# A fused attention and feed-forward kernel: eight of tile 3's twelve gate and val chunks as seven half-size products, with the program behind the opening written out in a new order

## The chip, the cores and the metric

The kernel runs on one core of a Trainium2 chip. The metric is the time of one execution in device microseconds (us); shown are 3 runs of the kernel before, from 216.14 to 217.49, with a median of 216.69. The time covers everything from the inputs in DRAM to the output in DRAM. Besides the times there is one execution recorded by the hardware profiler; its span, from the first to the last instruction, is shorter than the time, because start and end of the program are outside it.

## The reference

Attention with a decay per head, in blocks of 64 rows with a running state, then a gated feed-forward layer on its output:

```python
q, k, v: [4, 8, 768, 64]      lam: [8]         # batch, head, row, head_dim; fp32
for b in range(nb):                            # blocks of 64 rows, per batch and head
    intra = (qb @ kb.T * Dmask) @ vb           # Dmask = lam**(i-j) where i >= j, else 0
    inter = (qb * lam**(pos+1)) @ kv_state
    out[block] = intra + inter
    kv_state = lam**64 * kv_state + (kb * lam**(63-pos)).T @ vb
x = out, with heads side by side               # [3072, 512]
g = x @ w_gate;  v = x @ w_val                 # [3072, 1536]
result = (g * sigmoid(g) * v) @ w_out          # [3072, 512]
```

## The kernel before

**Tiles, groups, chunks.** The 3072 tokens are six tiles of 512 (t = 0 to 5). A tile is two groups, and a group is 256 rows of one batch; group g belongs to tile g // 2, and its state goes on to the group of the same batch four later. The attention of group g writes half of `xt` of its tile (bf16, d_model on the partitions). The feed-forward part of a tile cuts d_ff = 1536 into twelve chunks of 128 (`FC` = 12, two halves of `FH` = 6): for each chunk a gate product (L585) and a val product (L603), four pieces of d_model each, then SiLU on ScalarE (L590) and the product `h = sil * val` on VectorE (L607). Then the output product with `w_out` follows.

**Seven products instead of eight.** Where a matrix product is cut into two by two quarters, it can be had from seven products of quarters instead of eight, with sums of quarters made ahead and sums of results made behind. The kernel does so for the output product of tiles 1 to 5 (`out_units`, L805; its products `p1` to `p7`, L834 to L865, all matmuls at L823) and for the gate and val products of tiles 4 and 5 (`ffn_unit`, L716). The sums ahead are

- sums of the weights: `w_combo` (L681, the operation at L696), for gate and val n = 0, 1, 2, in `ws`; n = 3 overwrites a quarter of the weights in place, so after it no ordinary product can use that quarter. Sums of `w_out`: `wo_combo` (L644);
- sums of x: `x_combo` (L702, the operation at L714), four for a tile, three into `xs`, the fourth in place in `xt`;
- sums of h: `h_combo` (L655, the operation at L670), four for the chunks that are done, three into `hs`, one in place in `h`.

A call `ffn_unit(t, j, bk, ...)` makes four chunks at once: 2j, 2j+1 and the two six further on. Its seven products come one behind the other, each for gate (i = 0) and then for val (i = 1); a group of products is four matmuls of 256 columns at L733, so a unit has 7 x 2 x 4 = 56. It works in six of the eight PSUM banks, called A, E and B in pairs. The steps:

```python
        for i in range(2):
            product(i, A[i], wa(0, 0), xb(0, 0), True)
            nc.scalar.copy(out=Bb[i], in_=A[i])
        for i in range(2):
            product(i, E[i], wa(0, 1), xb(0, 1), True)
            nc.scalar.copy(out=es[i], in_=E[i])
        for i in range(2):
            product(i, Bb[i], wsum(1), xsum(1))
            nc.vector.tensor_tensor(out=E[i], in0=Bb[i], in1=es[i], op=ALU.add)
```

Then the product on A with `xb(1, 0)` and its SiLU; the product on B with `wsum(0), xsum(0)` and the addition of B and `es` into `es` (L783); the product on E with `xsum(2)`; the product on B with `wsum(2)`. The copies are L767 and L770, the additions L775 and L783, the SiLU L760, and `mult` (L763) makes h, three times on VectorE and once on GpSimd. So a group on E may begin only when its bank has been copied to `es` by ScalarE and rewritten by VectorE's addition.

**The attention of a group**, in steps which are functions: loads of q, k and v on SyncE's queue (`load_fp32`); `cast_scaled` (L287: k to bf16 on ScalarE, q times its decay factor on VectorE, and then `dma_transpose`, L276, which issues on SyncE's queue the DMA that transposes both into `qkt`); `v_scale` (L263: v times a decay factor, GpSimd or VectorE); `scores` (L362, L392) with masks on VectorE (L369, L397) that are collected in `later`; `upd_mm` (L424), `upd_copy` (L446, ScalarE) and `state` (L479 to L483, GpSimd) for the running state; `inter` (L518), `guard` (L502) and `intra` (L531) for the output of the group; `evac` (L544, L547) from PSUM to `xt`. The matmuls of scores, state and output are of 64 rows, those of the feed-forward part of 128.

**What sets the order.** The program is written in one order, and each engine runs its instructions in that order. The opening (groups 0 and 1 and the start of tile 0) is written out. Behind it `steps` lists the chunks tile by tile, `plan` (filled by `at`) hangs attention steps, loads and sums behind chosen chunks, and three lists hand out small work: `later` (masks), `trickle` by `drip` (sums of h, x and weights), and `kvq` by `kv_flush` (copies of the state). Tile 1 runs in halves of 256 columns, and so do the first four chunks of tile 2; chunks 4 and 5 of tile 2 are `HALVED`, each product split in two. Tile 3 takes its chunks in the order 0, 1, 6, 7, 2, 3, 8, 9, 4, 5, 10, 11, all twelve as ordinary chunks of 512 columns. `WS` (L1131) places the sums of the weights: two behind late chunks of tile 1, two in tile 2, and those with n = 2 and n = 3 in tile 3. The four sums of x for tile 4 are handed out during the output product of tile 2. From L1201 to the end the tail is written out: output of tile 2, units (4,0) and (4,1) with the attention of groups 10 and 11 in and between them, output of tile 3, unit (4,2), units (5,0) and (5,1), output of tile 4, unit (5,2), output of tile 5.

**Buffers.** The eight PSUM banks are given by a ring (`bank`, with `set_bank` and `fixed`). The pools touched: `raw` 10 (raw loads, sums of h, weight sums of the output), `qk` 3, `qkt` 3 (also sums of x of tile 4), `v` 4, `h` 5, `sil` 4, `osb` 4, and four `ups`/`es` buffers of 128 x 512 fp32.

## Time and profile before

| | us |
|---|---|
| median of the runs (216.14 to 217.49) | 216.69 |
| span of the profiled execution | 215.0 |
| VectorE busy | 148.3 |
| ScalarE busy | 130.9 |
| GpSimd busy | 92.7 |

Busy time of each engine by stretch of the span (us). PE is TensorE's matmuls; the stretches are, in turn: the opening, tile 0 and most of tile 1; the end of tile 1, first chunks of tile 2 and, from 69.3, the output product of tile 0 with the attention of group 5; tile 2 with the output product of tile 1; tile 3; the output product of tile 2 with units (4,0) and (4,1) and their attention, then the output product of tile 3; the units (4,2), (5,0), (5,1), (5,2) and the output products of tiles 4 and 5.

| stretch | length | PE | VectorE | ScalarE | GpSimd |
|---|---|---|---|---|---|
| 0 to 60 | 60.0 | 56.64 | 34.18 | 40.78 | 36.34 |
| 60 to 82 | 22.0 | 21.84 | 18.10 | 9.24 | 14.55 |
| 82 to 108 | 26.0 | 25.98 | 17.99 | 13.86 | 16.68 |
| 108 to 135.4 | 27.4 | 27.40 | 21.87 | 20.36 | 11.00 |
| 135.4 to 168.7 | 33.3 | 33.30 | 28.49 | 21.77 | 9.48 |
| 168.7 to 215 | 46.3 | 42.97 | 27.72 | 24.93 | 4.66 |

A row of the timeline or of the groups names engine, line, operation, the output and the inputs by the program's names, and partitions x elements; PE's ends are modelled, so its starts are the safer figure. Matmuls overlap: the time from one group's start to the next group's start is what a group costs.

### The profile page before, as it was taken

How to read it: one execution, taken by the hardware profiler on the slowest of the kernel's cores; microseconds unless marked ns; L12 is line 12 of the kernel's file. 1: busy time of each engine (PE TensorE's matmuls, PEld its weight loads, DVE VectorE, ACT ScalarE, POOL GpSimd, SP SyncE). 2: the span in 40 equal slices, each digit the busy share in tenths (PEclk: the TensorE clock that was granted, in tenths of full speed). 3: DMA queues.
4: the chain of work that ended last, by engine and by line, in shares of the span. 5: the costliest groups of instructions: out<-in, count | busy, mean ns of one | idle time of the engine just before them, and what ended most of it. 6: DMA issues, size and time to landing. Idle time of an engine off the chain costs nothing.

```text
span 215.0 us, 6856 instructions
## 1 busy us (share of the span) xinstructions
PE 208.1 (97%) x2797; PEld 153.3 (71%) x2801; DVE 148.3 (69%) x267; ACT 130.9 (61%) x280; POOL 92.7 (43%) x128
## 2 busy tenths in 40 slices
PE   8789999999999999999999999999999999999993
PEld 3467445887888548866754545888888888888883
DVE  1773447576677989874569878697988389961940
ACT  5878676756636153638369487774983676636522
POOL 6675755818399440595962153240750022200200
PEclk9999999999999999999999999999999999999999
DMA  6999999999999778899576859855000500005014
GB/s 188 345 354 381 376 336 296 285 226 223 309 387 174 185 212 208 244 214 263 122 198 143 217 121 257 207 121 201 5 3 5 195 0 3 0 0 198 0 52 146
DMA packets 82176, 39.76 MB, mean 185 GB/s; under 512 B 45410, under 2 KB 77794, under 8 KB 82146
## 3 DMA queue, kind: packets, MB, share of 16 engines
q1 hardware_dynamic: 80946, 38.74, 64.7%
q10 hardware_dynamic: 1200, 0.59, 0.9%
q8 instruction: 22, 0.36, 0.7%
q14 instruction: 8, 0.07, 0.1%
HBM read 28.31 MB, written 6.29 MB: 161 GB/s over the span
## 4 chain that ended last, share of the span: by engine, by line
PE 93%; DMA 2%; DVE 1%; SPq 1%; ACT 0%; issue 0%; DVEq 0%
PE bank L823 22%; PE bank L585 20%; PE bank L603 19%; PE bank L733 17%; PE bank L623 5%; PE bank L531 3%; DMA kraw<-in_k_dram 2%; PE bank L518 2%; PE bank L424 2%; PE bank L362 1%; DVE ssb L369 1%; SPq L115 1%; PE bank L392 1%; PE bank L322 1%; ACT qk L306 0%
## 5 line engine op out<-in xcount | busy, mean ns | idle before, releaser
L607 DVE TENSOR_TENSOR h<-sil,bank 128x256 bf16<-128x256 bf16 (+1 forms) x67 | 35.0, 533 | 29.9 <-PE bank L603 17.2
L585 PE MATMUL bank<-xt,wg_sb 128*128 128x256 bf16 (+1 forms) x276 | 52.8, 315 | 0.0
L603 PE MATMUL bank<-xt,wv_sb 128*128 128x256 bf16 (+1 forms) x276 | 52.5, 314 | 0.0
L590 ACT ACTIVATE sil<-bank 128x256 bf16<-128x256 f32 (+1 forms) x67 | 31.6, 481 | 21.8 <-PE bank L585 18.4
L603 PEld LDWEIGHTS <-wv_sb 128*128 128x128 bf16 x276 | 26.9, 98 | 14.8 <-POOL wv_sb L249 0.2
L585 PEld LDWEIGHTS <-wg_sb 128*128 128x128 bf16 x276 | 25.9, 98 | 13.6 <-issue 0.2
L266 POOL TENSOR_TENSOR v_s<-v,dec 128x512 bf16<-128x512 f32 (+1 forms) x18 | 23.0, 1295 | 24.3 <-DMA v<-in_v_dram 17.3
L763 POOL TENSOR_TENSOR h<-sil,es 128x512 bf16<-128x512 bf16 x6 | 7.0, 1165 | 47.4 <-ACT sil L760 47.4
L823 PEld LDWEIGHTS <-h 128*128 128x128 bf16 x240 | 23.3, 98 | 3.4 <-issue 0.3
L823 PE MATMUL bank<-wo_sb,h 128*128 128x256 bf16 x180 | 21.5, 273 | 0.0
L823 PEld LDWEIGHTS <-hs 128*128 128x128 bf16 x180 | 17.6, 98 | 2.7
L369 DVE TENSOR_TENSOR ssb<-bank,causal 128x512 bf16<-128x512 f32 x24 | 15.4, 684 | 1.8 <-PE bank L362 1.8
L479 POOL TENSOR_TENSOR kvf<-kvs,ups 128x256 f32<-128x256 f32 x8 | 6.5, 814 | 20.9 <-ACT ups L446 20.9
L733 PEld LDWEIGHTS <-ws 128*128 128x128 bf16 x144 | 13.8, 98 | 1.8
L823 PE MATMUL bank<-wt,hs 128*128 128x256 bf16 x120 | 15.0, 273 | 0.0
L775 DVE TENSOR_TENSOR bank<-bank,es 128x512 f32<-128x512 f32 x12 | 7.8, 694 | 9.6 <-PE bank L733 9.6
L479 POOL TENSOR_TENSOR kvf<-kvf,ups 128x256 f32<-128x256 f32 x16 | 13.0, 815 | 0.9
L760 ACT ACTIVATE sil<-bank 128x512 bf16<-128x512 f32 x18 | 10.5, 596 | 3.7 <-PE bank L733 3.7
L733 PE MATMUL bank<-xs,ws 128*128 128x256 bf16 x96 | 12.6, 273 | 0.0
L763 DVE TENSOR_TENSOR h<-sil,bank 128x512 bf16<-128x512 bf16 x18 | 11.8, 683 | 0.3 <-ACT sil L760 0.3
L623 PE MATMUL bank<-wo_sb,h 128*128 128x512 bf16 x45 | 10.7, 380 | 0.2
L733 PE MATMUL bank<-xt,wg_sb 128*128 128x256 bf16 x72 | 10.8, 273 | 0.0
(119 smaller groups left out, 360.3 us busy)
## 6 DMA issues: line engine op xcount, KB each, us to landing
out_dram<-osb SPq DMA_DIRECT2D x22, 256.0 KB, 2.6
v<-in_v_dram SPq DMA_DIRECT2D x18, 256.0 KB, 4.6
woraw<-in_moe_w_out_dram SPq DMA_DIRECT2D x6, 512.0 KB, 7.1
kraw<-in_k_dram SPq DMA_DIRECT2D x24, 128.0 KB, 3.4
qraw<-in_q_dram SPq DMA_DIRECT2D x24, 128.0 KB, 3.4
wraw<-in_moe_w_gate_dram SPq DMA_DIRECT2D x5, 512.0 KB, 6.9
wraw<-in_moe_w_val_dram SPq DMA_DIRECT2D x5, 512.0 KB, 7.0
kraw<-in_k_dram SPq DMA_DIRECT2D x4, 512.0 KB, 6.3
```

The lines of the kernel that those rows point to most:

```text
L266: eng.tensor_tensor(out=st[("vs", g)][:, h0:h1], in0=st[("v", g)][:, h0:h1].rearrange("p h (s d) -> p h s d", s=2), in1=vfac(g, h0, h1), o ...
L369: nc.vector.tensor_tensor(out=ssb[:, h2, 2 * c:2 * c + 2].rearrange("p a s n -> p a (s n)"), in0=sp[(c, h2)].rearrange("p (a x) -> p a x", ...
L479: nc.gpsimd.tensor_tensor(out=o, in0=f, in1=u, op=ALU.add)
L585: nc.tensor.matmul(gp[:, n0:n1], wg_sb[:, mc, fs], xt[:, g0:g1, mc].rearrange("p g b n -> p g (b n)"), start=(mc == 0 and n0 == 0), stop=( ...
L590: nc.scalar.activation(sil[:, 0:N], gp[:, 0:N], AF.Silu)
L603: nc.tensor.matmul(vp[:, n0:n1], wv_sb[:, mc, fs], xt[:, g0:g1, mc].rearrange("p g b n -> p g (b n)"), start=(mc == 0 and n0 == 0), stop=( ...
L607: nc.vector.tensor_tensor(out=h_sb[:, fc % FH, b0:b1].rearrange("p b n -> p (b n)"), in0=sil[:, 0:N], in1=vp[:, 0:N], op=ALU.mult)
L623: nc.tensor.matmul(ps, st[("h", t, fc // FH)][:, fc % FH, b], wo_sb[:, fc, c0:c1], start=(fc == 0), stop=(fc == FC - 1))
L733: nc.tensor.matmul(o[:, fi * 256:fi * 256 + 256], lhs(i, c, 2 * j + fi), rhs(c), start=(start and fi == 0 and c == 0), stop=(c == KH - 1), ...
L760: nc.scalar.activation(sil[key], src, AF.Silu)
L763: eng.tensor_tensor(out=h_of(half, r), in0=v3(sil[half, r]), in1=v3(src), op=ALU.mult)
L823: nc.tensor.matmul(o, lhs(f), rhs(f), start=(start and f == 0), stop=(f == FH - 1), skip_group_check=True)
```

## The change

**Tile 3.** Chunks 0, 1, 6, 7 and 2, 3, 8, 9 become units (3,0) and (3,1) of seven products; 4, 5, 10, 11 stay ordinary. So `ws` of all three kinds and the overwriting n = 3 for these chunks must be done before tile 3, and tile 3 gets sums of x, the fourth into a place of its own since ordinary chunks of the tile still read `xt`:

```diff
-    XS0 = 4
+    XS0 = (3, 4)
...
-            xs[t] = pool.tile([128, 3, 2, KH, BLK], BF16, name="xs", tag=tag)
+            xs[t] = pool.tile([128, 4 if t == 3 else 3, 2, KH, BLK], BF16, name="xs", tag=tag)
...
-    HALVED = ((2, 4), (2, 5))
+    HALVED = ((2, 10), (2, 11))
```

**Small functions.** `ffn_unit` and `out_units` are taken apart, so that each product group can stand anywhere in the program: `unit(t, j, bk)` names the banks, `uprod(t, j, k, i)` is product k for gate or val with the copy or addition that belongs to it, `silu` and `mu` are its SiLU and multiplication; `out_new`, `oprod` and `store` do the same for the output product; `cast_scaled` becomes `kcast`, `qcast` and `dma_transpose`, `h_combo` becomes `hsum` (k = 0 to 3), `core_a`, `core_b` and `attend` become `op_new`, `inter`, `guard`, `intra` and `evr`; `mask` and `kvc` are single steps. `hsum`, `x_combo` and `w_combo` take an engine:

```diff
+    def uprod(t, j, k, i):
...
+        o, lhs, rhs = ((A, wa(0, 0), xb(0, 0)), (E, wa(0, 1), xsum(3) if t == 3 else xb(0, 1)), (Bb, wsum(1), xsum(1)),
+                       (A, wa(1, 0), xb(1, 0)), (Bb, wsum(0), xsum(0)), (E, wa(1, 1), xsum(2)),
+                       (Bb, wsum(2), xb(1, 1)))[k]
...
+        if k == 0:
+            nc.scalar.copy(out=Bb[i], in_=A[i])
+        if k == 1:
+            nc.scalar.copy(out=es[i], in_=E[i])
+        if k == 2:
+            nc.vector.tensor_tensor(out=E[i], in0=Bb[i], in1=es[i], op=ALU.add)
+        if k == 4:
+            nc.vector.tensor_tensor(out=es[i], in0=Bb[i], in1=es[i], op=ALU.add)
```

**The order.** `steps`, `plan`, `at`, `trickle` and the tail go, and everything behind the opening is a list of calls; `use(...)` names the banks of the next step. Tile 2 now runs chunks 6 to 9 in halves first, then 10 and 11 (halved products), then 0 to 5. The sums of the weights all move ahead of tile 3. The casts of q of groups 6 and 11 go to GpSimd, the cast of k of group 7 and the v scaling of group 6 to VectorE. From the end of tile 2 to the output of tile 2:

```diff
+    use(4, 5); op_new(7)
+    use(0, 1); scores(8)
+    inter(7, True)
+    use(6, 7); upd_mm(8)
...
+    use(2); ffn_gate(2, 5, 0, 4)
+    intra(7, False)
+    state(8)
+    evr(7, 1, ACTC)
+    w_combo(1, 3, (0, 2))
+    mask(8, 0, 0)
+    evr(7, 0, DVEC)
+    mask(8, 0, 1)
+    x_combo(3, 0, None)
+    x_combo(3, 3, None)
+    use(7); ffn_val(2, 5, 0, 4)
+    x_combo(3, 1, None, nc.gpsimd)
+    hsum(2, 0, 0, 4, 0, 2)
+    unit(3, 0, (0, 1, 5, 3, 4, 2))
+    uprod(3, 0, 0, 0)
+    uprod(3, 0, 0, 1)
+    uprod(3, 0, 1, 0)
+    uprod(3, 0, 3, 0)
+    silu(3, 0, 0, 0)
+    x_combo(3, 2, None)
+    uprod(3, 0, 2, 0)
+    uprod(3, 0, 1, 1)
+    uprod(3, 0, 2, 1)
+    kcast(9)
+    uprod(3, 0, 4, 0)
+    qcast(9, nc.vector)
+    dma_transpose(9)
...
+    uprod(3, 0, 3, 1)
+    uprod(3, 0, 4, 1)
+    uprod(3, 0, 5, 1)
+    uprod(3, 0, 5, 0)
...
+    mu(3, 0, 1, 1, nc.gpsimd)
+    v_scale(9, nc.gpsimd, 0, 4)
+    hsum(2, 1, 0, 4, 0, 2)
+    mu(3, 0, 0, 0)
+    uprod(3, 0, 6, 0)
...
+    unit(3, 1, (0, 5, 6, 3, 4, 7))
+    uprod(3, 1, 0, 0)
+    uprod(3, 1, 0, 1)
+    uprod(3, 0, 6, 1)
+    uprod(3, 1, 1, 0)
...
+    mu(3, 1, 0, 1)
+    hsum(2, 2, 4, 6, 0, 2)
+    hsum(2, 2, 0, 4, 0, 2)
+    use(3, 2); op_new(8)
+    use(6); ffn_gate(3, 4, 0, 4)
+    inter(8, True)
...
+    use(4, 5); scores(9)
+    use(0, 1); upd_mm(9)
+    kcast(10)
...
+    qcast(10, nc.vector)
+    use(7); ffn_val(3, 4, 0, 4)
+    dma_transpose(10)
...
+    use(2, 5); scores(10)
```

Unit (3,0) so has an order of its own: product 3 for gate stands before product 2, and product 2 for gate before product 1 for val. In the units of tiles 4 and 5 the order of the products stays much as it was; the sums of h and x and the additions around them move, some to GpSimd.

More of the change, by code (lines that the diff above doesn't have):

```diff
@@ new lines, in oprod @@
+        for f in range(FH):
+            nc.tensor.matmul(o, lhs(f), rhs(f), start=(k in (1, 7) and f == 0), stop=(f == FH - 1),
+                             skip_group_check=True)
+        if k == 1:
+            act(out=Bb, in_=A)
+        if k == 7:
+            act(out=es, in_=E)
+        if k == 2:
+            act(out=O[0][:, 0:HD], in_=A)
+        if k == 6:
+            nc.vector.tensor_tensor(out=E, in0=Bb, in1=es, op=ALU.add)
+        if k == 5:
+            nc.vector.tensor_tensor(out=O[1][:, HD:DM], in0=Bb, in1=es, op=ALU.add)
@@ new lines, in _body @@
+    w_combo(0, 0, (0, 3))
+    use(2); ffn_gate(2, 9, 0, 2)
+    use(6); ffn_val(2, 9, 0, 2)
+    w_combo(1, 0, (0, 3))
+    wo_combo(1)
+    use(4); ffn_out(0, 0)
+    use(5, 6); op_new(5)
+    inter(5, True)
+    kcast(6)
+    guard(5)
+    use(7, 0, 1, 2); scores(5)
+    mask(5, 1, 1)
+    mask(5, 1, 0)
+    mask(5, 0, 1)
+    mask(5, 0, 0)
+    use(3); ffn_out(0, 1)
+    intra(5, False)
+    qcast(6, nc.gpsimd)
+    evr(5, 0, DVEC)
+    dma_transpose(6)
+    load_fp32(7, nc.sync, k, "kraw")
@@ new lines, in _body @@
+    store(1, 0, 0, 0, 512, None)
+    w_combo(1, 1, (0, 3))
+    w_combo(0, 2, (0, 3))
+    w_combo(0, 3, (0, 2))
+    use(4); ffn_val(2, 1, 0, 4)
+    use(5, 6); op_new(6)
+    inter(6, True)
+    guard(6)
+    use(7, 0); upd_mm(7)
+    upd_copy(7)
+    use(3, 2); scores(7)
+    intra(6, False)
+    state(7)
+    v_scale(8, nc.gpsimd, 0, 4)
+    use(1); ffn_gate(2, 2, 0, 4)
+    w_combo(1, 2, (0, 3))
+    mask(7, 0, 0)
+    use(7); ffn_val(2, 2, 0, 4)
+    kcast(8)
+    mask(7, 0, 1)
+    evr(6, 0, DVEC)
@@ new lines, in _body @@
+    hsum(3, 1, 0, 4, 0, 2)
+    unit(4, 0, (2, 4, 3, 5, 6, 7))
+    uprod(4, 0, 0, 1)
+    uprod(4, 0, 0, 0)
+    uprod(4, 0, 1, 1)
+    uprod(4, 0, 1, 0)
+    uprod(4, 0, 2, 0)
+    uprod(4, 0, 2, 1)
+    use(0, 1); scores(11)
+    mask(11, 0, 1)
+    uprod(4, 0, 3, 0)
+    silu(4, 0, 0, 0)
+    uprod(4, 0, 3, 1)
+    uprod(4, 0, 4, 0)
+    uprod(4, 0, 4, 1)
+    uprod(4, 0, 5, 1)
+    mu(4, 0, 0, 0)
+    silu(4, 0, 1, 1)
+    uprod(4, 0, 5, 0)
+    silu(4, 0, 1, 0)
+    mask(11, 0, 0)
+    use(2, 1); op_new(10)
```

1175 lines of the change are left out of this document (714 added, 461 removed).

## The prediction

> **What bounds the kernel now.** I read the page first, then the chain of waits in order of time, then the waits of TensorE, then the shapes of each line, and last the timeline around a seven-product unit.
>
> ```profile
> span 215.0 us, 6856 instructions
> PE 208.1 (97%) x2797; PEld 153.3 (71%) x2801; DVE 148.3 (69%) x267; ACT 130.9 (61%) x280; POOL 92.7 (43%) x128
> PE   8789999999999999999999999999999999999993
> PEclk9999999999999999999999999999999999999999
> ```
>
> PE is busy 97% of the span, its clock is full throughout, and what is idle lies in the opening (the first slices) and in the last slice. The waits of PE over the span add up to 3.2 us in seven rows; asked for the stretch from 60 us to the end, the same view has no row. The chain of waits shows the pace:
>
> ```profile
> 97.47 0.38 PE bank L518 x32
> 97.84 0.27 PE bank L424 x30
> 98.11 0.32 PE bank L392 x31
> 98.43 0.32 PE bank L531 x32
> 98.75 0.97 PE bank L585 x4
> 99.71 0.86 PE bank L603 x4
> ...
> 113.60 0.86 PE bank L585 x4
> 114.47 0.86 PE bank L603 x4
> 115.33 0.86 PE bank L585 x4
> ...
> 168.68 18.43 PE bank L733 x168
> ```
>
> An ordinary chunk of 512 columns is four gate and four val products of 0.216 us each: 113.60 to 115.33 is 1.73 us, wall to wall. The last row is three units of tiles 4 and 5: 168 products of 256 columns in 18.43 us, 0.110 us each. So PE streams without pause, and only two things can move the end: fewer columns on PE, or a wait that is not there now. The built order of the two kernels is the same on PE up to the scores of group 4 (about 60 us here), so the opening and its waits stay, and so does the 3.3 us between the last product and the end. The profiled execution took 215.0 us; the median of the runs is 216.69, so 1.69 is added to every span below.
>
> **The change, part by part.**
>
> Columns on PE. Eight chunks of tile 3 cost 8 x 1.73 = 13.84 us. They become two units of 56 products: 2 x 18.43/3 = 12.29 us. Saved: 1.55 us. That the change really issues fewer columns is seen in its order: 64 products of 512 columns go, 112 of 256 come, every other PE shape keeps its count.
>
> One more switch. PE changes between full and 64-row products 56 times after, 54 before; a chunk behind such a block takes 0.97 instead of 0.86 (98.75 against 113.60). One more visit, in and out: 0.11 to 0.2, taken as 0.15.
>
> Work around the units. The rows I use:
>
> ```profile
> L770 ACT COPY es<-bank 128x512 f32<-128x512 f32 x12 | 6.6, 612 | 0.0
> L775 DVE TENSOR_TENSOR bank<-bank,es 128x512 f32<-128x512 f32 x12 | 7.8, 694 | 9.6 <-PE bank L733 9.6
> L763 POOL TENSOR_TENSOR h<-sil,es 128x512 bf16<-128x512 bf16 x6 | 7.0, 1165 | 47.4 <-ACT sil L760 47.4
> ```
>
> and from the timeline of a unit of tile 4 (start, us, engine, line, operation):
>
> ```profile
> 168.51 0.60 PE L733 MATMUL bank<-xt,wg_sb 128*128 128x256 bf16 x4
> 168.95 0.60 PE L733 MATMUL bank<-xt,wv_sb 128*128 128x256 bf16 x4
> 169.21 1.06 ACT L767 COPY bank<-bank 128x512 f32<-128x512 f32 x2
> ```
>
> In the first three, the figure behind the comma is the mean in ns. A product group of four takes 0.44 (168.51 to 168.95); its reader starts 0.10 after its modelled end (169.11 to 169.21), so 0.26 after the next group has begun. A DVE operation that follows another directly costs its duration less 0.08 to 0.09.
>
> VectorE loses eight h products (8 x 0.685) and gains, for two units, six multiplications of 0.683 and eight additions of 0.69, a net gain of work of 4.1 us; with three sums of x for tile 3 and what is passed between engines, its rows add up to about 6 more on 148. GpSimd takes two casts of q (1.9 each), four sums of x, three of h and one of weights, and two multiplications of 1.17, and gives up 4.2 of v scaling. Sums on GpSimd are in no row here; the nearest is the 1165 ns row (same 512 elements), the ends are 0.72 (an addition of kvf, 256) and 2.1 (a v scaling of 1024), and I take 1.0 to 1.2. Together about 10 more on 93. ScalarE's rows add up to the same. No engine gets near PE, so none of this costs by amount; it costs by place.
>
> Place one, the way into unit (3,0). In tile 4 the sums of x run beside 84 products of output work (135.39 to 144.56). Now only one val group of 512 columns, 0.86 + 0.11, stands between the last product of group 7's attention and the unit. VectorE must evacuate (0.73), do a mask (0.60), and the first and fourth sum of x (0.35 each), 2.1 us with the reader's start; PE has 0.97 + 2 x 0.44 = 1.85 of other work until the third group, which reads the fourth sum. Wait: 0.3. The second sum, on GpSimd, starts at about 1.85 and takes about 1.17; the group that reads it comes at 3.0: no wait if GpSimd is free, else the whole excess.
>
> Place two, the order inside unit (3,0). The group with E's second half is followed by three groups, 1.32, before the one that must see it copied (0.61 on ScalarE), added (0.69) and released: 0.26 + 0.61 + 0.69 = 1.56. Wait: 0.25 to 0.4. In tile 4's order five groups lie between. The pair before it: 0.26 + 0.69 against 0.88, wait 0.1.
>
> Place three, unit (3,1). VectorE has in a row q's cast of group 9 (1.2), two additions, a sum of h and two multiplications (about 0.6 each) before the bank of E is free again: 0.26 + 4.2 against ten groups, 4.4, less the waits above. Wait: 0 to 0.3, taken 0.1.
>
> Together 0.8. The weight sums now fall beside tile 2's ordinary chunks; VectorE is busy 17.99 of 26.0 us between 82 and 108 us, and their 8 to 9 us mostly move within 82 to 135 us (21.87 of 27.4 in the second part), so I cost them at nothing; if that cover is gone, a bank is freed late and a chunk waits its 0.7. SyncE's order is the same before and after. Elsewhere PE's reordering finds nothing to remove.
>
> Sum on the span: 215.0 - 1.55 + 0.15 + 0.8 = 214.4, that is 216.1 beside the median.
>
> **A rule against the change.** The trace has the same sum of x at two prices (the line's own view, then two rows of the timeline):
>
> ```profile
> L714 DVE TENSOR_TENSOR xs<-xt,xs x4: 417/422/1197, 140.9 to 162.4; 128x512 bf16<-128x512 bf16 x4
> ...
> 142.32 1.20 DVE L714 TENSOR_TENSOR xs<-xt,xs 128x512 bf16<-128x512 bf16 x1
> 140.92 2.31 POOL L266 TENSOR_TENSOR v_s<-v,dec 128x512 bf16<-128x512 f32 x2 [5.02 <-DMA v<-in_v_dram]
> ```
>
> The slow one starts while GpSimd scales v and ends 0.3 after it. A sum of h at 78.18 took 2.27 instead of 0.55 beside another v scaling. So a pair of these costs 0.8 to 1.7 more for one of them. The Trainium skill, "SBUF — State Buffer", section "Who interferes with whom", says that a VectorE operation with two SBUF inputs and a GpSimd operation that reads SBUF lock each other out for a whole instruction. The trace agrees with it in these rows, and by that rule at place one the second sum of x could be held by a sum of h of 0.68, which would make the sum 215.1 and the time 216.8.
>
> **The rivals.** Main case: some of the gain is given back in waits of 0.3 to 1.9 us, spans 213.9 to 215.5, times 215.6 to 217.2. Chance 0.58.
>
> No wait shows, because ScalarE and VectorE keep ahead: 215.0 - 1.55 + 0.15 = 213.6, time 215.3, with a spread of 0.3% (the runs go from 216.14 to 217.49) 214.6 to 215.9. For it: PE waits nowhere after 60 us today, in five such units. Against it: places one and two are tighter than any in those five. Chance 0.20. Since no wait is left to remove there, a gain of over 1% would need more than the columns give.
>
> The other side: VectorE comes late out of unit (3,1), q of group 10 is cast late, and its transposing DMA lands late for the scores of group 10. From the unit's last product VectorE needs 0.26 + 0.68 + two sums of h, 1.0, + the cast, 1.3, and the DMA 3.8 from issue to landing (its median of nine), 7.1 in all; PE has 8.2 of work until those scores. It decides from a backlog of 1.1 us. Two GpSimd and VectorE collisions at 1.7 each make 3.4: waits of 0.8 + 3.4 in the units and the scores, span 215.0 - 1.4 + 4.2 = 217.8, time 219.5; one collision gives 217.8. For it: GpSimd's new work stands beside VectorE's sums in these units. Against it: most operations there read PSUM, and additions with a PSUM input beside GpSimd kept their 0.69. Chance 0.21.
>
> Half-size products might not be cheaper at all; the 0.110 against 0.216 leaves that no room, chance 0.01. The Trainium skill, "TensorE: Matmul & The Clock Gate", section "Back-to-back issue gap", gives a sustained 131 ns for 512 columns and 81 for 128; with some 98 for 256, an estimate between these, 112 against 64 products would lose 2.6 us. The trace disagrees: 0.216 us, in a stream with weight loads.
>
> **How the numbers follow.** About 1% is what a measurement of this kernel can tell from no change: 214.5 to 218.9. Faster by over 1%: a third of the no-wait case, 0.06. Slower by over 1%: the upper two thirds of the late case, 0.14. Within: 0.80. Prediction 216.1. The range 214.8 to 218.6 takes in the main case, most of the no-wait case and the lower part of the late one.
>
> **What would show it.** In the profile after: two more units at 6.1 us each if they run free, so the stretch of tile 3's units tells the waits directly; PE idle at the third group of unit (3,0) behind VectorE's sum of x (place one), before its last group on the second bank pair behind the additions (place two); sums of x on GpSimd well over 1.2 us (the lock); the scores of group 10 waiting for a transposed qkt (the late case). The prediction is wrong if PE waits somewhere before the units, where I put nothing, or if PE's stream itself has another pace.

## The result, and the profile after

Seven runs of the changed kernel took 217.43 to 220.92 us, median 218.47, beside a median of 216.69 for the kernel before; the ratio is 1.0067, with a 95% interval of 1.004 to 1.0094. So the change makes the kernel slower by about 0.7%, where 0.3% faster was forecast. The profiled execution took 217.71 us with a span of 215.7. The page after:

```profile
span 215.7 us, 6978 instructions
PE 208.7 (97%) x2845; PEld 158.5 (74%) x2849; DVE 157.5 (73%) x276; ACT 132.0 (61%) x282; POOL 106.5 (49%) x137
PE   8889999999999999999999999999999999999994
PEclk9999999999999999999999999999999999999998
```

The clock falls only in the last slice, behind the last product. GpSimd works 106.5 us instead of 92.7, VectorE 157.5 instead of 148.3, and PE still looks full. A wait of 0.1 to 0.5 us hardly shows in a page or in the view of waits, since the ends of matmuls are modelled. So below, a wait of PE is the time from one matmul's start to the next one's, beyond 0.109 us for 256 columns or 0.216 for 512. From the first product of unit (3,0), 111.84, to the first gate product of chunk 4, 125.40, this gives 13.56 us, of which 1.36 are waits; what is left, 12.20, is 0.109 for each of 112 products, beside the 12.29 that were forecast for them. The table further down adds the 0.13 that the first product of the unit waits, 1.5 in all.

The way into unit (3,0) and its first products, in the timeline after (start, us, engine, line):

```profile
110.99 0.73 DVE L531 CAST xt<-bank 128x512 bf16<-128x512 f32 x1 [0.48 <-PE bank L513]
111.63 0.67 DVE L358 TENSOR_TENSOR ssb<-bank,causaln 128x512 bf16<-128x512 f32 x1
111.84 0.60 PE L715 MATMUL bank<-xt,wg_sb 128*128 128x256 bf16 x4
112.22 1.05 DVE L679 TENSOR_TENSOR xs<-xt 128x512 bf16<-128x512 bf16 x2
112.35 0.60 PE L715 MATMUL bank<-xt,wv_sb 128*128 128x256 bf16 x4
113.01 1.27 POOL L679 TENSOR_TENSOR xs<-xt,xs 128x512 bf16<-128x512 bf16 x1 [0.36 <-DVE xs L679]
...
113.32 0.60 PE L715 MATMUL bank<-xs,wg_sb 128*128 128x256 bf16 x4 [0.38 <-DVE xs L679]
113.79 1.04 DVE L632 TENSOR_TENSOR hs<-h 128x1024 bf16<-128x1024 bf16 x1
...
115.46 0.59 ACT L721 COPY es<-bank 128x512 f32<-128x512 f32 x1 [0.37 <-PE bank L715]
116.08 0.70 DVE L723 TENSOR_TENSOR bank<-bank,es 128x512 f32<-128x512 f32 x1 [0.30 <-ACT es L721]
...
116.83 0.60 PE L715 MATMUL bank<-xs,ws 128*128 128x256 bf16 x4
```

Evacuation, mask and two sums of x follow each other on VectorE and are through at 113.27; the third product group starts at 113.32, 0.54 late. The copy, the addition and then a product, 115.46 to 116.83, are place two.

In the output product of tile 2, TensorE waits 0.48 us for an addition (L785):

```profile
141.75 1.90 POOL L282 TENSOR_TENSOR qk<-qraw,qdn 128x1024 bf16<-128x1024 f32 x1 [1.98 <-DMA qraw<-in_q_dram]
141.78 2.15 DVE L632 TENSOR_TENSOR hs<-h 128x512 bf16<-128x512 bf16 x1
...
143.85 0.41 DVE L785 TENSOR_TENSOR osb<-bank,osb 128x256 f32<-128x256 f32 x1
...
144.32 0.82 PE L774 MATMUL bank<-wo_sb,hs 128*128 128x256 bf16 x6 [0.31 <-DVE osb L785]
```

A sum of h that takes 0.42 elsewhere starts 0.03 after GpSimd's cast of q and ends 0.28 after it; the addition is queued behind it. At the scores of group 10 TensorE waits 0.27 us, and the profile shows two ends there within 0.1 us: ScalarE's evacuation of their bank, and the landing of their `qkt`, for which the weight load waits:

```profile
132.64 0.72 ACT L531 CAST xt<-bank 128x512 bf16<-128x512 f32 x1
133.41 0.34 PEld L383 LDWEIGHTS <-qkt 64*64 64x64 bf16 x32 [0.19 <-DMA qkt<-qk]
```

And the stretch of SyncE's queue from the transposing DMA of group 9 to that of group 11, with the scores of group 11 behind:

```profile
118.64 1.63 SPq L268 DMA_TRANSPOSE qkt<-qk  x1
120.32 2.69 SPq L124 DMA_DIRECT2D kraw<-in_k_dram  x4
123.11 2.05 SPq L116 DMA_DIRECT2D qraw<-in_q_dram  x4
125.27 1.01 SPq L124 DMA_DIRECT2D v<-in_v_dram  x2
129.66 1.67 SPq L268 DMA_TRANSPOSE qkt<-qk  x1
131.38 1.07 SPq L755 DMA_DIRECT2D out_dram<-osb  x2
132.49 3.45 SPq L124 DMA_DIRECT2D kraw<-in_k_dram  x4
135.99 2.10 SPq L116 DMA_DIRECT2D qraw<-in_q_dram  x4
...
143.68 1.59 SPq L268 DMA_TRANSPOSE qkt<-qk  x1
...
147.70 0.45 PE L383 MATMUL bank<-qkt 64*64 64x64 bf16 x32
```

The steps form a chain: the loads of group 10 stand in the queue behind the transposing DMA of group 9 (here T9), the casts of group 10 wait for them, T10 for the casts, and so on to T11. The same steps in the kernel before, with the casts of q and k of group 11 ahead of T11:

```profile
115.92 1.63 SPq L279 DMA_TRANSPOSE qkt<-qk  x1
...
128.06 1.67 SPq L279 DMA_TRANSPOSE qkt<-qk  x1
...
139.77 1.21 DVE L293 TENSOR_TENSOR qk<-qraw,qdn 128x1024 bf16<-128x1024 f32 x1
141.06 1.04 ACT L291 CAST qk<-kraw 128x1024 bf16<-128x1024 f32 x1
142.13 1.60 SPq L279 DMA_TRANSPOSE qkt<-qk  x1
...
146.24 0.45 PE L392 MATMUL bank<-qkt 64*64 64x64 bf16 x32
```

T9, T10 and T11 are issued 2.7, 1.6 and 1.55 us later after the change. For T11, the cast of q of group 11 begins 1.98 later (141.75 against 139.77), since it waits for its raw data, and takes 0.69 longer, on GpSimd instead of VectorE; 1.12 of this is taken up by the stretch between that cast and T11 in the kernel before, where ScalarE's cast of k still ran. In the recorded execution T11 lands 3.8 us after its issue, at about 147.5, and the scores start at 147.70: TensorE does not wait for it there.

### The profile page after: what moved, and what is told of

The parts are those of the page before. It is cut to its first block, busy times and chain, and to the rows that moved or that the text cites. A ratio compares the mean times of both kernels' runs of the same rounds, so it can differ in the third digit from the quotient of the medians.

```text
span 215.7 us, 6978 instructions
## 1 busy us (share of the span) xinstructions
PE 208.7 (97%) x2845; PEld 158.5 (74%) x2849; DVE 157.5 (73%) x276; ACT 132.0 (61%) x282; POOL 106.5 (49%) x137
## 4 chain that ended last, share of the span: by engine, by line
PE 92%; DVE 3%; ACT 2%; issue 1%; DVEq 0%
PE bank L715 23%; PE bank L774 20%; PE bank L559 17%; PE bank L577 16%; PE bank L597 5%; PE bank L513 3%; PE bank L500 2%; PE bank L408 2%; PE bank L347 1%; DVE ssb L362 1%; PE bank L310 1%; PE bank L383 1%; PE bank L182 1%; PE bank L148 1%; DVE xs L679 1%
## 5 line engine op out<-in xcount | busy, mean ns | idle before, releaser
L577 PE MATMUL bank<-xt,wv_sb 128*128 128x256 bf16 (+1 forms) x244 | 43.9, 306 | 0.0
L559 PE MATMUL bank<-xt,wg_sb 128*128 128x256 bf16 (+1 forms) x244 | 43.5, 306 | 0.0
L581 DVE TENSOR_TENSOR h<-sil,bank 128x256 bf16<-128x256 bf16 (+1 forms) x59 | 29.3, 512 | 19.2 <-PE bank L577 12.7
L564 ACT ACTIVATE sil<-bank 128x256 bf16<-128x256 f32 (+1 forms) x59 | 27.0, 462 | 18.7 <-PE bank L559 15.4
L577 PEld LDWEIGHTS <-wv_sb 128*128 128x128 bf16 x244 | 23.4, 98 | 9.7
L559 PEld LDWEIGHTS <-wg_sb 128*128 128x128 bf16 x244 | 22.9, 98 | 10.2 <-DVE xt L528 0.3
L260 POOL TENSOR_TENSOR v_s<-v,dec 128x512 bf16<-128x512 f32 (+1 forms) x15 | 18.3, 1234 | 7.7 <-DMA v<-in_v_dram 7.7
L715 PEld LDWEIGHTS <-ws 128*128 128x128 bf16 x192 | 18.5, 98 | 3.0 <-issue 0.4
L715 PE MATMUL bank<-xs,ws 128*128 128x256 bf16 x128 | 17.3, 272 | 0.0
L715 PEld LDWEIGHTS <-wg_sb 128*128 128x128 bf16 x128 | 12.4, 98 | 2.4 <-issue 0.6
L715 PEld LDWEIGHTS <-wv_sb 128*128 128x128 bf16 x128 | 12.4, 98 | 1.8 <-issue 0.2
L715 PE MATMUL bank<-xt,wv_sb 128*128 128x256 bf16 x88 | 13.2, 273 | 0.0
```

Of the source, the lines that this page charges most:

```text
L260: eng.tensor_tensor(out=st[("vs", g)][:, h0:h1], in0=st[("v", g)][:, h0:h1].rearrange("p h (s d) -> p h s d", s=2), in1=vfac(g, h0, h1), o ...
L559: nc.tensor.matmul(gp[:, n0:n1], wg_sb[:, mc, fs], xt[:, g0:g1, mc].rearrange("p g b n -> p g (b n)"), start=(mc == 0 and n0 == 0), stop=( ...
L564: nc.scalar.activation(sil[:, 0:N], gp[:, 0:N], AF.Silu)
L577: nc.tensor.matmul(vp[:, n0:n1], wv_sb[:, mc, fs], xt[:, g0:g1, mc].rearrange("p g b n -> p g (b n)"), start=(mc == 0 and n0 == 0), stop=( ...
L581: nc.vector.tensor_tensor(out=h_sb[:, fc % FH, b0:b1].rearrange("p b n -> p (b n)"), in0=sil[:, 0:N], in1=vp[:, 0:N], op=ALU.mult)
L715: nc.tensor.matmul(o[i][:, fi * 256:fi * 256 + 256], lhs(c, 2 * j + fi), rhs(c), start=(k < 2 and fi == 0 and c == 0), stop=(c == KH - 1), ...
```

## The experiments

Fifteen kernels, each timed in five rounds beside the kernel before. The table shows what the profiles gave: issue of T9 and T11, start of the scores of group 11, start of the last product (us), and the waits of PE in and around the two units. T9 and T11 are the transposing DMAs of groups 9 and 11. The times of a row are those of one execution; the ratio is that of all its runs.

| kernel | ratio, 95% interval | T9 | T11 | scores 11 | last product | at the units |
|---|---|---|---|---|---|---|
| before | | 115.9 | 142.1 | 146.2 | 211.4 | |
| changed | 1.0067, 1.004 to 1.0094 | 118.6 | 143.7 | 147.7 | 212.2 | 1.5 |
| e0 changed, again | 1.0084, 1.005 to 1.0119 | 118.5 | 143.9 | 148.3 | 212.7 | 1.6 |
| e1 no units | 1.0119, 1.0078 to 1.0159 | 116.7 | 144.1 | 150.6 | 215.0 | |
| e2 one visit | 1.0048, 1.0021 to 1.0075 | 118.3 | 144.0 | 148.3 | 212.7 | 1.4 |
| e3 sum behind | 1.0085, 1.0055 to 1.0115 | 120.2 | 145.2 | 149.6 | 214.1 | 1.5 |
| e4 q of 10 first | 1.0096, 1.0064 to 1.0127 | 119.6 | 143.9 | 150.4 | 214.8 | 1.5 |
| e5 casts back | 1.0055, 1.0025 to 1.0085 | 119.2 | 143.9 | 147.8 | 212.4 | 1.5 |
| e6 units eased | 1.0037, 1.001 to 1.0064 | 118.4 | 144.1 | 148.4 | 212.8 | 0.8 |
| e7 e5 and e6 | 1.0047, 1.002 to 1.0073 | 121.3 | 145.5 | 149.6 | 214.2 | 0.8 |
| e8 tile 2 eased | 1.0099, 1.0061 to 1.0137 | 118.3 | 143.7 | 148.0 | 212.5 | 1.5 |
| e9 all eased | 1.0018, 0.9997 to 1.0039 | 118.0 | 143.4 | 147.5 | 211.9 | 0.6 |
| e10 e9, no units | 1.0105, 1.0076 to 1.0134 | 115.4 | 145.7 | 149.4 | 213.9 | |
| e11 chain early | 0.9976, 0.9947 to 1.0005 | 116.6 | 142.6 | 146.6 | 211.1 | 0.9 |
| e12 e11, cast 9 back | 1.0020, 0.9993 to 1.0046 | 117.3 | 142.7 | 146.8 | 211.2 | 1.4 |
| b1 before, cast 9 one chunk later | 1.0076, 1.0046 to 1.0105 | 117.2 | 142.8 | 146.9 | 212.0 | |
| b2 before, two chunks later | 1.0196, 1.0155 to 1.0236 | 119.6 | 144.4 | 148.5 | 213.6 | |

**e1, the units undone.** `unit(3, 0)` and `unit(3, 1)` become eight ordinary chunks in the written-out order.

```diff
-    w_combo(1, 3, (0, 2))
...
-    unit(3, 0, (0, 1, 5, 3, 4, 2))
-    uprod(3, 0, 0, 0)
...
+    use(0); ffn_gate(3, 0, 0, 4)
+    use(1); ffn_val(3, 0, 0, 4)
...
+    w_combo(1, 3, (0, 2))
```

> The changed kernel with chunks 0, 1, 6, 7 and 2, 3, 8, 9 of tile 3 as ordinary chunks again, in the written-out order; the sums of x of tile 3 go, and the in-place sums of the weights move behind the chunks. Theory (the columns are saved as forecast, 1.55 us, and the waits in and around the two units, about 1.5 us in the profile of the changed kernel, give them back): 1.55 come back on the columns, 1.5 of waits go, the time stays that of the changed kernel, ratio to before 1.005 to 1.009. Rival (the units run nearly free, and the loss is the new order elsewhere): 1.5 us slower than the changed kernel, ratio to before 1.012 to 1.015.

1.0119 lies between the two, its interval takes in both, and the kernel is not clean: one of the moved weight sums holds masks, and so the state update of group 10, for 1.23 us, and the output product of tile 2 waits 1.11. Undoing the units does not bring the kernel back to the time before. Its median, 219.78, is 3.1 us above that of the kernel before, and less the 1.23 of its own it would still be some 1.9 above, an estimate: so part of the loss belongs to the order outside the units.

**e2, one visit for group 7.**

```diff
-    use(0, 1); scores(8)
     inter(7, True)
...
-    use(2); ffn_gate(2, 5, 0, 4)
+    use(0, 1); scores(8)
     intra(7, False)
     state(8)
+    use(2); ffn_gate(2, 5, 0, 4)
```

> The changed kernel with the attention of group 7 in one visit: output from the state, update, scores of group 8 and the intra part in one stretch, and the last gate and val of tile 2 both behind it. Theory (the way into unit (3,0) waits because only one val group, 0.97 us, covers the evacuation and the sums of x): the waits at the unit's first and third product group, 0.13 and 0.54 us, fall to under 0.2 together, a switch of 0.2 goes as well, 0.6 to 0.9 us faster than the changed kernel, ratio to before 1.002 to 1.005. Rival (VectorE's amount decides: both masks of group 8 now stand right ahead of the evacuation and the sums): the wait comes back whole, within 0.2 us of the changed kernel.

The wait at the third product group went, but a wait of 0.61 came at the first: ScalarE evacuates behind the SiLU of the chunk now ahead of it. The units' waits are 1.4, and at the scores of group 11 TensorE waits another 1.3. The runs' ratio is lower than that of the changed kernel, with intervals that overlap.

**e3, the sum of h behind the addition.**

```diff
-    hsum(3, 0, 4, 6, 0, 2)
     oprod(2, 1, 5)
+    hsum(3, 0, 4, 6, 0, 2)
```

> The changed kernel with one sum of h (tile 3, first kind, third pair) moved on VectorE behind the addition of the output product of group 5. Theory (that sum takes 2.15 instead of 0.42 us beside GpSimd's cast of q of group 11, and the addition queued behind it holds TensorE 0.48 us): that wait goes, 0.3 to 0.5 us faster than the changed kernel, ratio to before 1.004 to 1.006, and the moved sum is fast or is slow without harm. Rival (VectorE is behind by that much anyway, and the wait turns up at the next addition or in unit (4,0)): within 0.15 us of the changed kernel.

The wait at the addition is gone, the moved sum takes 1.83, and TensorE waits 0.84 at the scores of group 11 instead: the rival, a little further on.

**e4, q of group 10 first.** Two `hsum(2, 2, ...)` move behind `qcast(10)`.

> The changed kernel with VectorE's cast of q of group 10 ahead of two sums of h of tile 2, so that its transposing DMA is issued about 1.0 us earlier. Theory (the scores of group 10 wait 0.26 us for that DMA): the DMA is issued at about 128.6 instead of 129.66, the wait goes, 0.2 to 0.3 us faster than the changed kernel, ratio to before 1.005 to 1.006. Rival (ScalarE's cast of k and the queue set the issue, or the evacuation of group 8 is late behind the sums): within 0.1 us of the changed kernel, or a new wait of 0.3 to 0.7 at chunk 5 of tile 3.

The theory fell. The timeline of this kernel:

```profile
129.01 1.23 DVE L282 TENSOR_TENSOR qk<-qraw,qdn 128x1024 bf16<-128x1024 f32 x1 [0.80 <-DMA qraw<-in_q_dram]
...
132.88 1.02 PE L577 MATMUL bank<-xt,wv_sb 128*128 128x512 bf16 x4 [0.75 <-DVE h L581]
```

The cast does not start earlier, because the raw q of group 10 lands only then; the sums, now behind it, hold an h product and TensorE 0.9 us. Nor was the DMA alone what the scores of group 10 waited for in the changed kernel: ScalarE's evacuation ends at 133.36, and they start at 133.42. In e11, where the first weight load shows that `qkt` had landed at least 0.4 us before, they wait 0.40 for ScalarE.

**e0, e5, e6, e7.** The changed kernel again; `qcast(6)` and `qcast(11)` on VectorE with `v_scale(6)` on GpSimd; the units' neighbourhood; both. The core of e6:

```diff
-    x_combo(3, 0, None)
     x_combo(3, 3, None)
+    x_combo(3, 0, None)
+    x_combo(3, 1, None)
     use(7); ffn_val(2, 5, 0, 4)
-    x_combo(3, 1, None, nc.gpsimd)
...
+    banks[:] = [banks[p] for p in (3, 6, 5, 1, 4, 0, 2, 7)]
...
     uprod(3, 0, 1, 0)
+    uprod(3, 0, 1, 1)
+    uprod(3, 0, 2, 0)
+    uprod(3, 0, 2, 1)
...
     uprod(3, 0, 3, 0)
```

> The changed kernel once more, for a second profile and more times beside the same kernel before. Theory (fixed waits of about 1.5 us in and around the two units, the same in every profile, and waits that vary from execution to execution at chunk 9 of tile 2, at the scores of group 6 and around the output product of tile 2, where a cast of q on GpSimd and sums on VectorE hold each other): the waits of the units as in the first profile within 0.05 us each, the others together anywhere from 0.9 to 3 us, ratio to before 1.005 to 1.010. Rival (the first profile was typical and the others differ by their edits): every wait of the first profile again within 0.1 us.

> The changed kernel with the casts of q of groups 6 and 11 on VectorE instead of GpSimd (that of group 11 behind the sums of x, when its raw data has landed), and the v scaling of group 6 on GpSimd again, as before the change. Theory (a cast on GpSimd takes 1.9 us and holds the sum on VectorE that starts beside it, 2.2 instead of 0.4 to 0.6): the waits at chunk 9 of tile 2, at the scores of group 6 and in the output product of tile 2 or at the scores of group 11 go or fall to 0.3 in all, the waits of the units stay, 0.8 to 1.5 us faster than the changed kernel, ratio to before 1.000 to 1.004. Rival (VectorE is simply full there; it now has 2.4 us more and 1.2 less): the waits turn up at the same chunks, within 0.3 us of the changed kernel.

> The changed kernel with the units' neighbourhood rearranged and nothing else: the attention of group 7 in one visit with its evacuation queued ahead of the next SiLU, the sums of x of tile 3 all on VectorE and in the order in which they are read, the pairs of products of unit (3,0) in the order of the units of tiles 4 and 5, other banks for the units (so that unit (3,0) starts in banks that are free), and the sum of h (tile 2) behind the multiplication that frees the bank of E. Theory (the three places are what the units lose): the fixed waits of 1.5 us fall to 0.4 or less and one switch of 0.2 goes, 1.1 to 1.5 us faster than the changed kernel, ratio to before 1.000 to 1.003. Rival (VectorE's amount between 108 and 127 us decides, not its order): waits of over 1 us at other product groups, within 0.4 us of the changed kernel.

> Both edits together: the units' neighbourhood rearranged and the casts of q of groups 6 and 11 back on VectorE. Theory (two separate causes that add): 2 to 3 us faster than the changed kernel, ratio to before 0.994 to 0.998, and the saving on the columns, 1.55 us, is seen in the time. Rival (one follows from the other, or a third chain, the transposing DMAs of groups 10 and 11, takes over): no better than the better of the two alone, ratio 1.000 to 1.004, with waits for qkt of 0.3 us or more.

e0 repeats the units' waits (1.6 against 1.5), while the others differ, as the theory had it: none at the addition, but 1.13 at the scores of group 11. e6 halves the units' waits, and its profile ends no earlier than e0's. The scores of group 11 in e0, then T9, T11 and those scores in e6:

```profile
148.25 0.45 PE L383 MATMUL bank<-qkt 64*64 64x64 bf16 x32 [1.06 <-DMA qkt<-qk]
...
118.36 1.65 SPq L268 DMA_TRANSPOSE qkt<-qk  x1
...
144.08 1.60 SPq L268 DMA_TRANSPOSE qkt<-qk  x1
...
148.36 0.45 PE L383 MATMUL bank<-qkt 64*64 64x64 bf16 x32 [1.25 <-DMA qkt<-qk]
```

In these two executions the 0.86 that the units gave back went elsewhere: 0.63 to waits in tile 2 of e6, 0.4 more to a gate product at 131.79, and 0.2 more to the wait for T11. Over all runs e6 was 0.8 us faster, with a median of 218.03 beside 218.82 for e0, where its theory gave 1.1 to 1.5; so what it changed at the units does count. In the table the changed kernel, e0, e1, e2, e4, e5, e6 and e8 issue T11 at 143.7 to 144.1, whatever stands upstream, although T9 goes from 116.7 (e1) to 119.6 (e4). In e1 and e4 the scores start 6.5 later, behind waits of 1.1 at the addition L785; in the others 3.9 to 4.4 later. T11 itself takes 4.2 to 4.3 us to land where TensorE waits for it (e0, e2, e3, e6, e8) and 3.7 to 3.8 in the others of these kernels; what makes it slower no run shows, and it is about half of those waits. From the scores of group 11 to the last product it is 64.45 to 64.6 us in every variant of the changed kernel, e1 and e3 included (65.2 in the kernel before, where eight products more stand behind them).

One pattern goes through the profiles. Where GpSimd casts q of group 11 (the changed kernel, e0 to e4, e6, e8), TensorE waits either at the addition (0.48, 1.11, 1.12) or at the scores of group 11 (0.8 to 1.3). In the five kernels with the units where VectorE casts it and the sum of h stands behind the addition (e5, e7, e9, e11, e12), it waits at neither. (e10, without the units, has a VectorE cast that is late itself.)

e5 took away the wait at the addition and the one at the scores, and has one of 0.87 at chunk 9 of tile 2; e7 shows why that place moves about:

```profile
76.56 1.91 POOL L260 TENSOR_TENSOR v_s<-v,dec 128x1024 bf16<-128x1024 f32 x1 [5.33 <-DMA v<-in_v_dram]
76.74 2.81 DVE L282 TENSOR_TENSOR qk<-qraw,qdn 128x1024 bf16<-128x1024 f32 x1
...
88.48 0.83 DVE L278 CAST qk<-kraw 128x1024 bf16<-128x1024 f32 x1 [4.06 <-DMA kraw<-in_k_dram]
```

VectorE's cast of q, 1.2 us alone, takes 2.81 beside GpSimd's scaling of v, which e5 and e7 put back there. The transposing DMA of group 6 and the loads of group 7 behind it are late, and VectorE, which has the cast of k of group 7 in its queue since the change, waits 4.06 us for it with the h products behind; TensorE waits 2.56 in the scores of group 6. In runs, e5 and e7 have medians of 218.50 and 218.09 beside 218.82 for e0: less than their theories gave, and e7 is no better than e6.

**e8, e9, e10.** In e8 only the cast of k of group 7 goes to ScalarE and a weight sum behind an h product; e9 is e6, e8, `qcast(6)` and `qcast(11)` on VectorE, and the state copies of group 9 behind a SiLU; e10 is e9's order with ordinary chunks.

> The changed kernel with two steps of tile 2 moved: the cast of k of group 7 on ScalarE behind the copy of the state update, instead of on VectorE ahead of the h products, and the last sum of the output weights behind the h product of chunk 8 instead of ahead of that of chunk 6. Theory (VectorE, which works in order, waits 0.6 to 4.1 us for raw k of group 7 with the h products that free TensorE's banks queued behind it, and comes to them late through sums slowed beside GpSimd): the waits at chunk 9 of tile 2 and in the scores of group 6, 0 to 0.9 and 0 to 2.6 us in the profiles so far, are under 0.1 each; all others stay; on the mean 0.3 to 0.8 us faster than the changed kernel, ratio to before 1.002 to 1.006, with less spread. Rival (these waits only take up slack that the output product of tile 2 or the scores of group 11 then claim): the same time within 0.2 us and the wait there longer.

> All of it: the units' neighbourhood, the two steps of tile 2, the casts of q of groups 6 and 11 on VectorE, and the copies of the state of group 9 behind a SiLU of tile 3 instead of ahead of it. Theory (fixed waits at the units, waits in VectorE's and ScalarE's queue for DMAs and for GpSimd, and nothing else): waits behind 60 us of under 1.5 us in all, 2 to 3 us faster than the changed kernel, ratio to before 0.994 to 0.998. Rival (the chain of transposing DMAs and loads of groups 9 to 11 sets the pace there, whatever VectorE does): scores of group 10 or 11 wait 0.5 us or more, ratio 0.999 to 1.003.

> The eased order of the run with all of it, but with the eight chunks of tile 3 ordinary (6 to 9 first, then 0 to 3, so that the in-place sums of the weights can follow within the tile), no sums of x for tile 3, and q of group 9 cast two chunks into the tile. Theory (half-size products are worth the 1.55 us of their columns, less the waits that stay at the units, 0.3 to 0.8): 0.7 to 1.3 us slower than the run with all of it, ratio to before 0.999 to 1.003. Rival (the units gain nothing, and any gain over the changed kernel is the order): within 0.3 us of the run with all of it.

e8 is the rival's case: no wait in tile 2, and 1.19 at the scores of group 11. e9 gains 0.5% or more on the changed kernel, about half of what its theory gave, and its ratio is its rival's; it waits 1.5 us for the state copies of group 9, which I had put too late, and at the scores of group 10. e10 is slower than e9 by 1.0105 against 1.0018, 1.9 us, more than either case: the 1.55 of the columns, less the 0.6 that e9 waits at the units, and a wait of 1.28 of its own in the output product, where the cast of group 11 is late on VectorE. So the pair agrees with a gain from the half-size products, but does not separate it from e10's own wait: 1.9 less 1.28 leaves 0.6.

**e11, the chain early.** The core of the edit, against e9:

```diff
+    kcast(9)
+    qcast(9, nc.vector)
     uprod(3, 0, 3, 0)
...
-    kcast(9)
     uprod(3, 0, 4, 0)
-    qcast(9, nc.vector)
...
+    kvc(9, 0)
     use(6); ffn_gate(3, 10, 0, 4)
-    kvc(9, 0)
```

> The run with all of it, and more of the same in tile 3: the casts of k and q of group 9 ahead of the third pair of additions of unit (3,0), so that the transposing DMA of group 9 and the loads of group 10 behind it are issued about 1 us earlier; the state copies of group 9 split around the SiLU of chunk 10 instead of all behind it; two state copies of group 8 moved off the copy that frees E in unit (3,1). Theory (what is left is that groups 8 and 9 stand only three chunks apart in tile 3, so copies, casts and transposing DMAs of both run into ScalarE's, VectorE's and the queue's order): the 1.5 us of waits at the state products of group 9 and the scores of group 10 fall to 0.6 or less, the 0.5 us in the units to 0.2, 1 to 1.4 us faster than the run with all of it, ratio to before 0.995 to 0.998. Rival (three chunks are too short for this chain in any order): 1 us or more of waits there, ratio 1.000 to 1.002.

```profile
116.63 1.64 SPq L268 DMA_TRANSPOSE qkt<-qk  x1
...
128.64 1.68 SPq L268 DMA_TRANSPOSE qkt<-qk  x1
...
142.56 1.60 SPq L268 DMA_TRANSPOSE qkt<-qk  x1
...
146.65 0.45 PE L383 MATMUL bank<-qkt 64*64 64x64 bf16 x32
```

T11 is issued 1.1 us earlier than in the changed kernel and the last product starts 1.1 us earlier. Median 216.36 beside 216.73 of the kernel before, ratio 0.9976: faster than the changed kernel, and not clear of the kernel before, since the interval ends at 1.0005. The waits at the units, 0.9, are more than e9's 0.6, against the expectation; those at the state products of group 9 and the scores of group 10 fall from 1.5 to 0.64, as the theory had it. In e9 and in e11 T11 lands 0.3 us before the scores that read it, so the 0.8 by which e11's last product is earlier than e9's comes from these waits, 0.9 less against 0.3 more at the units, and not from T11.

**e12, b1, b2: the chain alone.** e12 puts the cast of group 9 back in e11. b1 and b2 leave the kernel before as it was and move one step:

```diff
-            at(sn[j], cast_scaled, g)
-            at(sn[j], load_group, g + 1)
+            at(sn[j + (1 if g == 9 else 0)], cast_scaled, g)
+            at(sn[j + (1 if g == 9 else 0)], load_group, g + 1)
```

> The best version with one part undone: the casts of k and q of group 9 stand behind the first addition of the fourth pair of products of unit (3,0) again, as in the changed kernel; all else stays. Theory (SyncE's queue is a chain: transposing DMA of group 9, loads of group 10, its cast, its transposing DMA, loads of group 11, its cast, its transposing DMA, scores of group 11; and from those scores to the last product it is 64.5 us in every profile): the transposing DMAs of groups 9, 10 and 11 are issued about 1.5, 0.8 and 0.8 us later than in the best version (118.0, 129.4, 143.4 against 116.6, 128.6, 142.6), the scores of group 11 start at 147.2 to 147.6 instead of 146.6, 0.6 to 1.0 us slower than the best version, ratio to before 1.000 to 1.003. Rival (the waits at product groups are what counts, and the cast of group 9 had only its own wait of 0.28 us): within 0.3 us of the best version.

> The kernel before, not the changed one, with the cast of group 9 and its transposing DMA, and the loads of group 10 behind it, one chunk later in tile 3 (1.73 us); no product moves and nothing else is added. Theory (the chain had 0.2 to 0.3 us of slack at the scores of group 11: the DMA is issued at 142.13, lands some 3.8 to 4.0 later, the scores start at 146.24): the transposing DMA of group 9 is issued at about 117.6, that of group 11 0.5 to 1.5 us later than in the kernel before, and TensorE waits for qkt at the scores of group 11 for the first time, 0.3 to 1.2 us, ratio to before 1.001 to 1.006. Rival (five chunks lie between, and the loads have slack): no wait, ratio 0.999 to 1.001.

> The kernel before with the same steps two chunks later (3.46 us). Theory: the transposing DMA of group 9 is issued at about 119.4, later than in the changed kernel; the scores of group 9 wait 0.5 to 1.0 us for it, the scores of group 11 1.5 to 3 us, ratio to before 1.006 to 1.014, so without one half-size product this is as slow as the changed kernel or slower. Rival (slack in the loads): only the wait at the scores of group 9, ratio 1.002 to 1.005.

b1, one chunk later:

```profile
117.23 1.64 SPq L279 DMA_TRANSPOSE qkt<-qk  x1
...
129.27 1.68 SPq L279 DMA_TRANSPOSE qkt<-qk  x1
...
133.04 0.45 PE L392 MATMUL bank<-qkt 64*64 64x64 bf16 x32 [0.68 <-DMA qkt<-qk]
```

T9 is 1.3 us later, T10 1.2 and T11 0.6, and this makes the kernel before as slow as the changed one, 1.0076, with no half-size product in tile 3. In the profile the last product is 0.6 later. The wait, 0.86 from start to start, came at the scores of group 10, not 11 as I had written, with another of 0.41 at a val product behind them; once they are paid, the scores of group 11 are not late any more. In b2 TensorE waits 0.87 at the scores of group 9, 1.06 for a scaled v and 0.59 at the scores of group 10. e12 did not do what was expected: without the waits ahead of it T9 came at 117.3, not 118.0. T11 and the last product are 0.1 us later than in e11, although the units wait 1.36 instead of 0.89:

```profile
121.65 0.60 PE L715 MATMUL bank<-xs,ws 128*128 128x256 bf16 x4 [1.00 <-DVE bank L723]
...
142.70 1.60 SPq L268 DMA_TRANSPOSE qkt<-qk  x1
```

This does not make the wait of 1.17 in a unit (from start to start; the row gives 1.00) free: e12's first unit product starts 0.35 earlier than e11's (111.12 against 111.47), its two units take 0.47 longer, and the 0.12 between them is still there at the last product. It does show that T9 0.7 us earlier brings T11 forward by only 0.14. The runs of e12, 1.0020, are above e11's with intervals that overlap, so e12 stays undecided.

## Why the prediction was wrong

**Columns and switch.** Right: 12.2 for the two units against 12.29; the split visit of group 7 cost the 0.2 of a way in and out. The trace after has 0.109 per product of 256 columns and 0.216 of 512, as before. The Trainium skill, "TensorE: Matmul & The Clock Gate", section "Back-to-back issue gap", gives a sustained 131 ns for 512, by which the smaller products would have lost time; the trace disagrees once more.

**Place one.** Mechanism right, size off: 0.89 (0.13 for the evacuation, 0.08, 0.54 for the fourth sum of x, 0.14 for the second) against 0.3. The two sums took 1.05 instead of 0.70, beside GpSimd's state additions, and GpSimd's own sum 1.27. **Place two**: 0.32 against 0.3 and 0.1. **Place three**: 0.28 against 0.1.

**The lock.** The Trainium skill, "SBUF — State Buffer", section "Who interferes with whom", lets a GpSimd operation and a VectorE operation with two SBUF inputs exclude each other. The rows above agree (0.42 became 2.15). I had looked for it at the second sum of x, and it was dearest where GpSimd took over the casts of q.

**The step that failed** is the one that puts nothing for waits outside the units: SyncE's order is the same before and after, so the sum has no term for the queue, and GpSimd's casts of q are counted by amount and in no place. In the recorded execution TensorE waits 1.5 us in and around the units instead of 0.8, 0.48 at the addition behind a sum of h that GpSimd's cast of q holds, and 0.27 at the scores of group 10: 0.7 by which the units' term was too small, and 0.75 that was put at nothing, together about 1.4 beside the 1.3 by which the span was over.

The queue is the other part. Its order is the same; the times are not. The cast of group 9 moved from a chunk into the middle of unit (3,0), so T9 is issued 2.7 us later, and T10 and T11 follow by 1.6 and 1.55, the latter with 0.69 for a cast that is slower on GpSimd. In the trace of before T11 was issued at 142.13 and took 3.7 to land, until about 145.9, and the scores started at 146.24: 0.4 us of slack that I could have read and did not. In the recorded execution of the changed kernel this chain costs nothing on top, because TensorE is late already; but the forecast span of 214.4, less 3.5 from the start of the last product to the end and 64.45 from the scores of group 11 to that product, needs those scores at about 146.4, and T11 landed 1 us later. In e0 the wait stands there, 1.13. My late case had this mechanism, for the cast of group 10 behind VectorE's backlog, and gave it 0.21; it came through group 9, the queue and the cast of q of group 11.

**The numbers.** 216.1 against 218.47 is 2.4 off: 1.3 in the span (215.7 against 214.4); 0.3 because time and span of the changed kernel lie 2.0 to 2.1 apart in each of its runs, where I had added 1.69; and 0.8 because this execution, 217.71, was below the median. The range, up to 218.6, just held the median, and that in part by luck: its upper part was meant for collisions in unit (3,1) and a late T10. The sign was wrong. GpSimd's and VectorE's amounts rose by more than forecast: 13.8 instead of about 10 (92.7 to 106.5), and 9.2 instead of about 6 (148.3 to 157.5).

**What stays open.** How the 0.7% divides between the units, GpSimd's cast of q and the chain cannot be said from these runs, since a wait at one place is slack at the next. A cast of q of group 11 back on VectorE with nothing else changed was not tried, and what sets T11 in e10 was not tried apart.

## What to carry to other kernels

When steps are moved, follow each DMA queue through the whole stretch, not only its order: issue, landing, consumer, and the next issue that waits for that consumer, and read the slack at the last consumer. Waits on such a path need not add up: what is taken out at one place can come back, in part or whole, where the latest chain ends, as at the scores of group 11 in e2 and e3. One profile is not enough to say so, since e0 and the first profile of the same kernel have different waits; compare the medians too. Work handed from one engine to another with idle time is not free if the two hold each other up, or if it takes longer there and stands in front of a DMA (1.90 against 1.21).

## What the runs showed of the hardware

VectorE and GpSimd hold each other in both directions: a sum of h of 0.42 took 2.15 beside a GpSimd cast of 1.90, a cast of q of 1.2 took 2.81 beside a v scaling of 1.91; the VectorE sum ended 0.28 after GpSimd's operation. The other way round, in e6 a GpSimd addition took 1.56 beside VectorE's cast of q, and 0.73 elsewhere:

```profile
87.20 0.73 POOL L462 TENSOR_TENSOR kvf<-kvs,ups 128x256 f32<-128x256 f32 x1 [2.22 <-ACT ups L430]
...
128.15 1.23 DVE L282 TENSOR_TENSOR qk<-qraw,qdn 128x1024 bf16<-128x1024 f32 x1 [0.54 <-PE bank L577]
128.40 1.56 POOL L462 TENSOR_TENSOR kvf<-kvs,ups 128x256 f32<-128x256 f32 x1 [2.07 <-ACT ups L430]
```

An addition with one input in PSUM kept its 0.41 to 0.43. From the issue of T11 to the scores that read it were 3.8 to 4.4 us in the profiles where those scores waited or just did not.
